# Moving the DMA transposes of a convolution-plus-SwiGLU kernel from ScalarE to SyncE, in sixths of a block

## The chip, the cores and the metric

The kernel runs on one core of a Trainium2 chip. The metric is device time in microseconds (us) of one execution, median of several runs. Before the change it is 1375.94 us (2 runs, 1375.61 to 1376.27).

Engines as the profile names them: PE is TensorE's matmul, PEld its weight load, ACT is ScalarE, DVE VectorE, POOL GpSimd, SP SyncE. A "q" at the end (SPq, ACTq) is the engine's sequencer, which issues DMAs and waits on semaphores.

## The reference, cut to what matters

```python
B, S, D = 8, 4096, 192; H, K = 8, 7          # 8 heads of 24 channels, 7 taps; Dff = 1536
w = softmax(weight)                          # (H, K)
y[b, s, h, :] = sum_k w[h, k] * x_pad[b, s + k, h, :]      # causal depthwise conv, per head
g, v = y @ w_gate, y @ w_val                 # (32768, 192) @ (192, 1536)
out = (g * sigmoid(g) * v) @ w_out           # (32768, 1536) @ (1536, 192)
```

## The kernel before

The work goes in units of 1024 tokens, two blocks of 512 each; there are 32 units. The FFN of a block runs over 12 chunks of 128 hidden channels, so a unit has 24 chunks, numbered s = 0 to 23. Each chunk has six gate/val matmuls ("gv", contraction over 192 channels in three parts of 64), a silu on ScalarE, a multiply on VectorE giving `h`, and, a few chunks later, matmuls of the down projection ("f2"). The f2 or conv matmuls of one chunk are called a burst. Between two bursts stands a relay: a nop on SyncE that waits for the last matmul before it and releases the first matmul of the next burst.

The conv of the next unit is done on TensorE as a Toeplitz matmul in four phases between the chunks. Its result stands with tokens on partitions, but gv needs channels on partitions. So it is staged in SBUF, written to DRAM, and read back with DMA transposes into `xq`.

```python
def emit_relay():                                  # orders TensorE bursts that swap PSUM banks
    relay[0] = nc.sync.nop(nofuse=True)            # SyncE waits for the last matmul of a burst;
    tc.add_manual_dep(relay[0].ins, last_mm[0].ins.name, SYNC, ...)
                                                   # the next burst's first matmul waits for this nop
# ... cut ...
def emit_to_dram(u):
    st = conv.pop(u)
    nc.gpsimd.tensor_copy(st[:, :, D:XD], st[:, :, 0:Q])
    dr = tc.dram_tile([2 * UG * G, XD], fp16, name=f"xc{u}")     # UG, G = 9, 57; XD = 256
    for i, lo in enumerate((0, Q)):
        nc.gpsimd.dma_start(                                      # 57 partitions x 9 rows of 512 B
            out=dr[i * UG * G : (i + 1) * UG * G, :].rearrange("(g r) d -> r g d", r=G),
            in_=st[lo : lo + G])
    return dr

def emit_transpose(dr):
    xq = xpool.tile([P, NQ, UT], fp16, tag="xq", name="xq")
    for q in range(NQ):                                           # 3 transposes of 1024 rows a unit
        nc.scalar.dma_start_transpose(out=xq[:, q, :], in_=dr[0:UT, q * Q : q * Q + P])
    return xq
# ... cut; in the chunk loop:
    emit_h(emit_gv(j, xqs[u], (b % UB) * TB), hlists[b])          # gv, silu, multiply
    if not tail: emit_f2(fj % 2, (c, c + 1), accs[fb], hlists[fb])  # one burst in every chunk
    if s in (4, 5, 8, 9): emit_conv(u + 1, s // 8, s % 2)
    emit_relay()
    if s == 9:  dr = emit_to_dram(u + 1)
    if s == 15: xqs[u + 1] = emit_transpose(dr)                   # on ScalarE's queue
```

## Time and profile before

| what | value | how it was read |
|---|---|---|
| span | 1378.4 us | page |
| unit period | 42.00 us | first write to DRAM of one unit to that of the next, mean of 30 |
| ScalarE stop in each unit | 12.0 to 14.1 us (31 stops) | timeline |
| first gate matmul | 41.8 us | timeline |
| mean granted TensorE clock | 0.861 | cores |

The timeline of ScalarE, last chunks ahead of the stop (start, duration, engine and line, operation, tiles; in brackets the idle time before and what ended it):

```profile
649.64 0.60 ACT L259 ACTIVATE sig<-gate 128x512 f16<-128x512 f32 x1 [0.44 <-PE gate L248]
650.17 0.48 ACT L298 COPY o_sb<-acc_8237 128x384 f32<-128x384 f32 x1
650.62 0.60 ACT L259 ACTIVATE sig<-gate 128x512 f16<-128x512 f32 x1
660.20 4.55 ACTq L237 DMA_TRANSPOSE xq<-xc_8416  x3
664.85 1.08 ACT L259 ACTIVATE sig<-gate 128x512 f16<-128x512 f32 x2 [13.64 <-issue]
```

ScalarE computes nothing from 651.2 to 664.9 us. Its queue is in order, and in front of the next silu stand three transposes. The chain of waits for the same stretch says why they started only at 660.2 us:

```profile
646.67 1.55 POOL xc_8416 L228
648.22 0.18 issue
648.40 11.74 DMA xc_8416<-stage
660.14 0.03 ACTq L237
660.17 0.04 issue
660.20 1.18 ACTq L237
661.38 0.03 issue
661.41 1.99 ACTq L237
663.39 0.03 issue
663.42 1.33 ACTq L237
```

They wait 11.7 us for the write to DRAM. The three issues then take 1.18, 1.99 and 1.33 us. TensorE runs dry behind this. The windows view of the same stop gives the granted clock in the column PEclk (ahead of it the busy time of PE, PEld, DVE, ACT, POOL; after it the DMA share and GB/s):

```profile
651.00:664.00 13.00, 2.44 (x35) 1.87 (x35) 1.02 (x2) 0.22 (x1) 2.57 (x4) 0.69 0.79 126
664.00:667.00 3.00, 1.36 (x5) 0.40 (x6) 1.28 (x2) 1.08 (x2) 0.00 (x0) 0.50 0.93 154
667.00:670.30 3.30, 3.30 (x32) 2.49 (x30) 1.14 (x2) 1.19 (x2) 0.00 (x0) 0.60 0.02 5
670.30:675.00 4.70, 4.70 (x70) 3.75 (x68) 2.98 (x5) 2.86 (x5) 0.00 (x0) 1.00 0.00 0
```

The clock is at half speed from 656.0 us, and back at 1.00 from 669.7 us. The Trainium skill, "TensorE: Matmul & The Clock Gate", section "What's actually happening", describes this: the clock falls to half after an idle window of about 3.4 us, and comes back after about as long a busy stretch. The trace agrees only in part. Full speed is back 4.1 us after the matmuls resumed at 665.5 us. But half speed began 2.1 us after the last matmul before the stop (653.9 us), too early for a whole idle window of 3.4 us.

### The profile page before, as it was taken

The page shows a single profiled execution, that of the slowest core. Times are in us where ns is not written, and L with a number is a line of the kernel's source. Part 1 is how long each engine was busy: PE and PEld are TensorE (multiplying, and loading weights), DVE is VectorE, ACT ScalarE, POOL GpSimd, SP SyncE. Part 2 cuts the span into 40 slices and gives each one's busy share as a digit, 9 for nine tenths or more (in the row PEclk, how much of TensorE's full clock was granted, in tenths as well). Part 3 has the DMA queues.
Part 4 walks back from the last instruction along what each step waited for, and adds up shares of the span by engine and source line. Part 5 has one row for each costly group of instructions (what it writes and reads, how often), then busy time and mean ns, then how long its engine had stood idle before and what let it go on. Part 6 is the DMA issues. An engine that isn't in the chain of part 4 may idle for free.

```text
span 1378.4 us, 28477 instructions
## 1 busy us (share of the span) xinstructions
PE 930.9 (68%) x11760; PEld 680.5 (49%) x11760; DVE 559.4 (41%) x857; ACT 536.8 (39%) x963; POOL 270.3 (20%) x310
## 2 busy tenths in 40 slices
PE   1676667866668766668666687666687666786668
PEld 0454445644446544456444465444465444554445
DVE  3343334433334433344333344333344333443335
ACT  0343334443334433344433344333344333443334
POOL 8211122202222101222012221012221112220110
PEclk9988888888889888898888898888998888888889
DMA  6324343234342243432343422344322444224421
GB/s 85 57 51 76 64 75 55 42 67 75 64 76 45 47 72 64 75 57 43 65 75 64 75 45 49 71 64 75 65 51 50 73 64 75 48 45 71 64 63 36
DMA packets 174418, 85.46 MB, mean 62 GB/s; under 512 B 162384, under 2 KB 165136, under 8 KB 174288
## 3 DMA queue, kind: packets, MB, share of 16 engines
q0 software_dynamic: 72768, 58.43, 22.4%
q10 hardware_dynamic: 101376, 25.18, 12.6%
q8 instruction: 92, 1.51, 0.4%
q14 instruction: 38, 0.31, 0.1%
q1 hardware_dynamic: 144, 0.03, 0.0%
HBM read 31.77 MB, written 41.98 MB: 54 GB/s over the span
## 4 chain that ended last, share of the span: by engine, by line
PE 39%; DMA 27%; issue 15%; ACTq 11%; DVE 5%; POOL 2%; ACT 2%; POOLq 0%; DVEq 0%; SPq 0%
PE val L248 17%; ACTq L237 11%; PE gate L248 7%; DVE h L261 2%; ACT sig L259 2%; DVE o_sb L299 1%; DMA xc_10122<-stage 1%; DMA xc_5574<-stage 1%; DMA xc_1026<-stage 1%; DMA xc_12964<-stage 1%; DMA xc_3868<-stage 1%; DMA xc_15238<-stage 1%; DMA xc_7848<-stage 1%; DMA xc_458<-stage 1%; DMA xc_8416<-stage 1%
## 5 line engine op out<-in xcount | busy, mean ns | idle before, releaser
L248 PE MATMUL gate<-xq,w_sb 64*128 64x512 f16 x2304 | 697.6, 403 | 369.5 <-ACT sig L259 349.5
L261 DVE TENSOR_TENSOR h<-sig,val 128x512 f16<-128x512 f16 x768 | 520.9, 686 | 809.0 <-ACT sig L259 776.1
L259 ACT ACTIVATE sig<-gate 128x512 f16<-128x512 f32 x768 | 455.2, 597 | 780.4 <-issue 413.2
L248 PE MATMUL val<-xq,w_sb 64*128 64x512 f16 x2304 | 667.8, 399 | 19.3 <-DVE h L261 14.9
L248 PEld LDWEIGHTS <-w_sb 64*128 64x128 f16 x4608 | 335.6, 98 | 518.9 <-issue 446.9
L274 PEld LDWEIGHTS <-h 64*128 64x128 f16 x6112 | 435.3, 98 | 151.7 <-issue 85.5
L300 POOL DMA_DIRECT2D out_dram<-o_sb x64 | 50.0, 781 | 831.8 <-ACT sig L259 672.3
L203 PEld LDWEIGHTS <-toep 64*128 64x128 f16 x1024 | 63.1, 95 | 20.6 <-DVE toep L150 17.8
L225 POOL COPY stage<-stage 128x576 f16<-128x576 f16 x32 | 21.7, 677 | 110.8 <-ACT stage L216 110.8
L203 PE MATMUL cps_171<-x_0_82,toep 64*128 64x216 f16 x8 | 2.0, 373 | 17.8 <-DMA wo_sb<-in_moe_w_out_dram 17.8
L95 POOL DMA_DIRECT2D x_1_84<-in_x_dram x16 | 12.4, 772 | 0.0
L97 POOL DMA_DIRECT2D x_1_84<-in_x_dram x16 | 11.8, 738 | 0.0
L97 POOL DMA_DIRECT2D x_0_82<-in_x_dram x16 | 11.4, 714 | 0.0
L101 POOL DMA_DIRECT2D x_1_84<-in_x_dram x16 | 9.3, 579 | 0.0
L101 POOL DMA_DIRECT2D x_0_82<-in_x_dram x16 | 9.1, 567 | 0.0
L259 ACT ACT_TABLE_LOAD x1 | 1.3, 1283 | 17.9 <-issue 17.9
L274 PE MATMUL acc_17072<-wo_sb,h 64*128 64x192 f16 x48 | 6.9, 273 | 0.5 <-DVE o_sb L299 0.5
L274 PE MATMUL acc_2292<-wo_sb,h 64*128 64x192 f16 x48 | 6.9, 273 | 0.5 <-DVE o_sb L299 0.5
L274 PE MATMUL acc_15368<-wo_sb,h 64*128 64x192 f16 x48 | 6.9, 273 | 0.5 <-DVE o_sb L299 0.5
L274 PE MATMUL acc_9682<-wo_sb,h 64*128 64x192 f16 x48 | 6.9, 273 | 0.5 <-DVE o_sb L299 0.5
L274 PE MATMUL acc_14230<-wo_sb,h 64*128 64x192 f16 x48 | 6.9, 272 | 0.5 <-DVE o_sb L299 0.5
L274 PE MATMUL acc_11956<-wo_sb,h 64*128 64x192 f16 x48 | 6.9, 272 | 0.5 <-DVE o_sb L299 0.5
(583 smaller groups left out, 1199.3 us busy)
## 6 DMA issues: line engine op xcount, KB each, us to landing
out_dram<-o_sb POOLq DMA_DIRECT2D x64, 384.0 KB, 4.1
x_0_82<-in_x_dram POOLq DMA_DIRECT2D x24, 192.0 KB, 10.8
x_1_84<-in_x_dram POOLq DMA_DIRECT2D x16, 216.0 KB, 10.9
x_1_84<-in_x_dram POOLq DMA_DIRECT2D x16, 192.0 KB, 11.2
x_0_82<-in_x_dram POOLq DMA_DIRECT2D x8, 216.0 KB, 11.1
w_sb<-in_moe_w_gate_dram POOLq DMA_DIRECT2D x12, 48.0 KB, 3.0
w_sb<-in_moe_w_val_dram POOLq DMA_DIRECT2D x12, 48.0 KB, 2.7
wo_sb<-in_moe_w_out_dram POOLq DMA_DIRECT2D x4, 144.0 KB, 3.6
```

The costliest lines, as they stand in the source:

```text
L95: nc.gpsimd.dma_start(out=x16[0:Q, :, :], in_=windows(t0, Q, UG))
L97: nc.gpsimd.dma_start(out=x16[Q:P, 0 : UG - 1, :], in_=windows(tb, Q, UG - 1))
L101: nc.gpsimd.dma_start(out=x16[Q : Q + last_rows, UG - 1, :], in_=x_flat[tl : tl + last_rows, :])
L203: mm = nc.tensor.matmul(conv["ps"][a][:, :, e, :], toep[lo : lo + Q, c * H + h, :], x16[lo : lo + Q, :, h * grp : (h + 1) * grp], start=(p ...
L225: nc.gpsimd.tensor_copy(st[:, :, D:XD], st[:, :, 0:Q])
L237: nc.scalar.dma_start_transpose(out=xq[:, q, :], in_=dr[0:UT, q * Q : q * Q + P])
L248: last_mm[0] = nc.tensor.matmul(ps[i], w_r[lo : lo + Q, q, ts(j, P)], xq[lo : lo + Q, q, t : t + TB], start=(q == 0), stop=(q == NQ - 1),)
L259: nc.scalar.activation(sj, ps[0], AF.Silu)
L261: nc.vector.tensor_tensor(hj, sj, ps[1], op=ALU.mult)
L274: mm = nc.tensor.matmul(acc[a][:, i, :], hlist[j][lo : lo + Q, ts(2 * a + i, P)], wo_r[lo : lo + Q, j, :], start=(j == 0 and half == 0 and ...
L299: nc.vector.tensor_copy(o_sb[:, 2:4, :], acc[1])
L300: nc.gpsimd.dma_start(out=out[t0 : t0 + TB, :].rearrange("(s p) d -> p s d", p=P), in_=o_sb)
```

## The change

Its intent is to take the wait and the issue of the transposes off ScalarE, to write and transpose block by block and earlier, and to shorten the start. A block is transposed in six pieces of 256 rows, called sixths; thirds and twelfths, further down, are pieces of 512 and 128 rows. The diff, cut to its core:

```diff
-    F2_LAG = 3
+    TR = 3                      # down projection in chunk triples: a burst in 2 of 3 chunks
+    F2_LAG = TR + 1
+    RP = TB // 2                # 256 rows a transpose
 # ... start: weights through SyncE's hardware queue as fp32, cast on ScalarE and GpSimd;
 #     Toeplitz matrix in two halves; Silu table loaded early ...
+        dr = tc.dram_tile([UG * G, XD], fp16, name=f"xc{b}")      # one DRAM tile a block
+        nc.sync.dma_start(out=dr.rearrange("(g r) d -> r g d", r=G),
+                          in_=conv[u][i * Q : i * Q + G])
+    def emit_transpose(b, i):                                     # i = 0 .. 5
+        r, q = i // NQ * RP, i % NQ
+        nc.sync.dma_start_transpose(
+            out=xqs[b][:, q, r : r + RP], in_=drs[b][r : r + RP, q * Q : q * Q + P])
 # ... in the chunk loop ...
-            if u + 1 < n_units and s in (4, 5, 8, 9):
-                emit_conv(u + 1, s // 8, s % 2)
+        if more and s in (0, 3, 6, 9):
+            emit_conv(u + 1, s // 6, s // 3 % 2)
+        if burst and live:
+            emit_relay()                                          # still a nop on SyncE
+        if g >= F2_LAG and fj == NCH - 2:
+            emit_store(fb, accs.pop(fb))                          # ahead of this chunk's multiply
+            if s in (3, 4, 9, 10):
+                emit_conv_out(u + 1, s // 6, s % 3)
+            if s in (11, 12):
+                emit_to_dram((u + 1) * UB + s - 11)
+            if 17 <= s < 17 + 2 * NQ:
+                emit_transpose((u + 1) * UB, s - 17)              # even block of the next unit
+        if live and s < 2 * NQ:
+            emit_transpose(u * UB + 1, s)                         # odd block of this unit
```

More of the change, by code (lines that the diff above doesn't have):

```diff
@@ L49 @@
     XD = D + Q
-    F2_LAG = 3
+    TR = 3
+    F2_LAG = TR + 1
+    RP = TB // 2
     SCALE = 1024.0
-    assert D == NQ * Q and NQ == 3
-    assert S % UT == 0 and UT <= 2 * UG * G and UT > (2 * UG - 1) * G
+    assert D == NQ * Q and NQ == 3 and UB == 2 and UG * G >= TB
+    assert S % UT == 0 and (UG - 1) * G < TB <= UG * G
     assert G + pad <= Q
-    assert NCH % 2 == 0 and H % 4 == 0 and 2 * UG * grp <= 512
+    assert NCH % TR == 0 and UB * NCH == 24 and H == 8 and 2 * UG * grp <= 512
     n_blocks = NT // TB
@@ L66 @@
     spool = ctx.enter_context(tc.tile_pool(name="stage", bufs=2))
-    xpool = ctx.enter_context(tc.tile_pool(name="xq", bufs=2))
+    xpool = ctx.enter_context(tc.tile_pool(name="xq", bufs=3))
     hpool = ctx.enter_context(tc.tile_pool(name="ffn", bufs=2))
@@ L72 @@
     apool = ctx.enter_context(tc.tile_pool(name="acc", bufs=1, space=bass.MemoryType.PSUM))
-    last_rows = UT - ((2 * UG - 1) * G - pad)
+    last_rows = TB - ((UG - 1) * G - pad)
     x16s = []
@@ L95, in emit_fetch @@
             nc.gpsimd.dma_start(out=x16[0:Q, :, :], in_=windows(t0, Q, UG))
-        tb = t0 + UG * G
+        tb = t0 + TB
         nc.gpsimd.dma_start(
@@ L103, in emit_fetch @@
         )
-    emit_fetch(0)
+    man = tc.manual_schedule(engines={EN.PE, EN.SP, EN.Activation, EN.DVE, EN.Pool})
+    ctx.enter_context(man)
     wraw = const_pool.tile([P, H, K], fp32, tag="wraw", name="wraw")
@@ L111 @@
     )
+    emit_fetch(0)
+    w_st = wpool.tile([P, NQ, Dff], fp32, tag="w_st", name="w_st")
+    wo_st = wpool.tile([P, NCH, D], fp32, tag="wo_st", name="wo_st")
+    w_r = wpool.tile([P, NQ, Dff], fp16, tag="w_sb", name="w_sb")
+    wo_r = wpool.tile([P, NCH, D], fp16, tag="wo_sb", name="wo_sb")
+    FS = Dff // 4
+    wg_v = moe_w_gate.rearrange("(q p) f -> p q f", p=Q)
+    wv_v = moe_w_val.rearrange("(q p) f -> p q f", p=Q)
+    wo_v = moe_w_out.rearrange("(c p) d -> p c d", p=P)
+    for f in range(0, Dff, FS):
+        fs = slice(f, f + FS)
+        cs = slice(f // P, (f + FS) // P)
+        nc.sync.dma_start(out=w_st[0:Q, :, fs], in_=wg_v[:, :, fs])
+        nc.sync.dma_start(out=w_st[Q:P, 0 : NQ - 1, fs], in_=wv_v[:, 1:NQ, fs])
+        nc.sync.dma_start(out=w_st[Q:P, NQ - 1, fs], in_=wv_v[:, 0, fs])
+        nc.sync.dma_start(out=wo_st[:, cs, :], in_=wo_v[:, cs, :])
+    diag = const_pool.tile([P, G], i32, tag="diag", name="diag")
+    for lo in (0, Q):
+        nc.gpsimd.iota(diag[lo : lo + Q], pattern=[[-1, G]], base=0, channel_multiplier=1)
+    band = const_pool.tile([P, H, 2, G], fp16, tag="band", name="band")
+    nc.gpsimd.memset(band, 0.0)
+    toep = const_pool.tile([P, H, 2, P], fp16, tag="toep", name="toep")
+    nc.gpsimd.memset(toep, 0.0)
+    masks = []
+    for k in range(K):
+        mask = const_pool.tile([P, G], u16, tag=f"mask{k}", name=f"mask{k}")
+        nc.vector.tensor_scalar(mask, diag, scalar1=k, scalar2=None, op0=ALU.is_equal)
+        masks.append(mask)
     wmax = const_pool.tile([P, H], fp32, tag="wmax", name="wmax")
@@ L118 @@
     nc.scalar.activation(wexp, wexp, AF.Exp)
+    warm = const_pool.tile([P, H, K], fp32, tag="warm", name="warm")
+    nc.scalar.activation(warm, wexp, AF.Silu)
     wsum = const_pool.tile([P, H], fp32, tag="wsum", name="wsum")
     nc.vector.tensor_reduce(wsum, wexp, axis=AX.X, op=ALU.add)
-    nc.vector.tensor_scalar(wsum, wsum, scalar1=1e-9, scalar2=None, op0=ALU.add)
+    nc.vector.tensor_scalar(
+        wsum, wsum, scalar1=1e-9, scalar2=1.0 / SCALE, op0=ALU.add, op1=ALU.mult
+    )
     nc.vector.reciprocal(wsum, wsum)
@@ L126 @@
     )
-    nc.vector.tensor_scalar(wn, wn, scalar1=SCALE, scalar2=None, op0=ALU.mult)
-    whl = const_pool.tile([P, 2, H, K], fp16, tag="whl", name="whl")
-    nc.vector.tensor_copy(whl[:, 0], wn)
-    nc.vector.tensor_tensor(whl[:, 1], wn, whl[:, 0], op=ALU.subtract)
-    diag = const_pool.tile([P, G], i32, tag="diag", name="diag")
-    for lo in (0, Q):
-        nc.gpsimd.iota(diag[lo : lo + Q], pattern=[[-1, G]], base=0, channel_multiplier=1)
-    band = const_pool.tile([P, 2 * H, G], fp16, tag="band", name="band")
@@ L137 @@
-    nc.gpsimd.memset(band, 0.0)
-    toep = const_pool.tile([P, 2 * H, P], fp16, tag="toep", name="toep")
-    nc.gpsimd.memset(toep, 0.0)
-    wflat = whl.rearrange("p c h k -> p (c h) k")
-    for k in range(K):
-        mask = const_pool.tile([P, G], u16, tag=f"mask{k}", name=f"mask{k}")
-        nc.vector.tensor_scalar(mask, diag, scalar1=k, scalar2=None, op0=ALU.is_equal)
-        nc.vector.copy_predicated(
-            band,
-            mask.unsqueeze(1).to_broadcast([P, 2 * H, G]),
-            wflat[:, :, k : k + 1].to_broadcast([P, 2 * H, G]),
-        )
@@ L150 @@
-    nc.vector.tensor_copy(toep[0:Q, :, 0:G], band[0:Q])
-    nc.vector.tensor_copy(toep[Q:P, :, Q : Q + G], band[Q:P])
-    w_r = wpool.tile([P, NQ, Dff], fp16, tag="w_sb", name="w_sb")
-    wo_r = wpool.tile([P, NCH, D], fp16, tag="wo_sb", name="wo_sb")
-    FS = Dff // 4
-    wo_v = moe_w_out.rearrange("(c p) d -> p c d", p=P)
-    for f in range(0, Dff, FS):
-        for lo, w, first in ((0, moe_w_gate, 0), (Q, moe_w_val, 1)):
-            wv = w.rearrange("(q p) f -> p q f", p=Q)
-            for q in range(NQ):
-                nc.gpsimd.dma_start(
-                    out=w_r[lo : lo + Q, q, f : f + FS],
-                    in_=wv[:, (q + first) % NQ, f : f + FS],
-                )
-        c0, c1 = f // P, (f + FS) // P
-        nc.gpsimd.dma_start(out=wo_r[:, c0:c1, :], in_=wo_v[:, c0:c1, :])
+    whl = const_pool.tile([P, H, 2, K], fp16, tag="whl", name="whl")
@@ new lines @@
+    nc.vector.tensor_copy(whl[:, :, 0], wn)
+    nc.vector.tensor_tensor(whl[:, :, 1], wn, whl[:, :, 0], op=ALU.subtract)
+    for h in range(0, H, 4):
+        hs = slice(h, h + 4)
+        for k in range(K):
+            nc.vector.copy_predicated(
+                band[:, hs].rearrange("p h c m -> p (h c) m"),
+                masks[k].unsqueeze(1).to_broadcast([P, 8, G]),
+                whl[:, hs, :, k : k + 1]
+                .rearrange("p h c k -> p (h c) k")
+                .to_broadcast([P, 8, G]),
+            )
+        nc.vector.tensor_copy(toep[0:Q, hs, :, 0:G], band[0:Q, hs])
+        nc.vector.tensor_copy(toep[Q:P, hs, :, Q : Q + G], band[Q:P, hs])
@@ L169, with emit_weight_cast @@
+    def emit_weight_cast(i):
+        fs = slice(i * FS, (i + 1) * FS)
+        cs = slice(i * FS // P, (i + 1) * FS // P)
+        nc.scalar.copy(w_r[:, :, fs], w_st[:, :, fs])
+        nc.gpsimd.tensor_copy(wo_r[:, cs, :], wo_st[:, cs, :])
+    emit_weight_cast(0)
     SYNC = mybir.DependencyInfo(mybir.DependencyClass.Sync, mybir.DependencyReason.DATA)
@@ L204, in emit_conv @@
                         conv["ps"][a][:, :, e, :],
-                        toep[lo : lo + Q, c * H + h, :],
+                        toep[lo : lo + Q, h, c, :],
                         x16[lo : lo + Q, :, h * grp : (h + 1) * grp],
@@ L211, in emit_conv, with emit_conv_out, emit_dup, emit_to_dram @@
                     after_relay(mm)
-    def emit_conv_out(u, fill):
-        for a in range(2):
-            d0 = (4 * fill + 2 * a) * grp
-            nc.scalar.mul(
-                conv[u][:, :, d0 : d0 + 2 * grp],
-                conv["ps"][a].rearrange("p g e d -> p g (e d)"),
-                1.0 / SCALE,
-            )
-    def emit_to_dram(u):
-        st = conv.pop(u)
-        nc.gpsimd.tensor_copy(st[:, :, D:XD], st[:, :, 0:Q])
-        dr = tc.dram_tile([2 * UG * G, XD], fp16, name=f"xc{u}")
-        for i, lo in enumerate((0, Q)):
-            nc.gpsimd.dma_start(
-                out=dr[i * UG * G : (i + 1) * UG * G, :].rearrange("(g r) d -> r g d", r=G),
-                in_=st[lo : lo + G],
-            )
-        return dr
-    def emit_transpose(dr):
-        xq = xpool.tile([P, NQ, UT], fp16, tag="xq", name="xq")
-        for q in range(NQ):
-            nc.scalar.dma_start_transpose(
-                out=xq[:, q, :], in_=dr[0:UT, q * Q : q * Q + P]
-            )
-        return xq
-    def emit_gv(j, xq, t):
+    def emit_conv_out(u, fill, a):
+        d0 = (4 * fill + 2 * a) * grp
+        nc.scalar.mul(
+            conv[u][:, :, d0 : d0 + 2 * grp],
+            conv["ps"][a].rearrange("p g e d -> p g (e d)"),
+            1.0 / SCALE,
+        )
+    def emit_dup(u):
+        nc.gpsimd.tensor_copy(conv[u][:, :, D:XD], conv[u][:, :, 0:Q])
+    drs = {}
+    def emit_to_dram(b):
+        u, i = divmod(b, UB)
+        dr = tc.dram_tile([UG * G, XD], fp16, name=f"xc{b}")
+        nc.sync.dma_start(
+            out=dr.rearrange("(g r) d -> r g d", r=G),
+            in_=conv[u][i * Q : i * Q + G],
+        )
+        drs[b] = dr
+    xqs = {}
+    def emit_transpose(b, i):
+        if i == 0:
+            xqs[b] = xpool.tile([P, NQ, TB], fp16, tag="xq", name="xq")
+        r, q = i // NQ * RP, i % NQ
+        nc.sync.dma_start_transpose(
+            out=xqs[b][:, q, r : r + RP], in_=drs[b][r : r + RP, q * Q : q * Q + P]
+        )
+    def emit_gv(j, xq):
         ps = [
@@ L250, in emit_gv @@
                     w_r[lo : lo + Q, q, ts(j, P)],
-                    xq[lo : lo + Q, q, t : t + TB],
+                    xq[lo : lo + Q, q, :],
                     start=(q == 0),
@@ L255, in emit_gv, with emit_silu, emit_h @@
         return ps
-    def emit_h(ps, hlist):
+    def emit_silu(ps):
         sj = hpool.tile([P, TB], fp16, tag="sig", name="sig", bufs=3)
         nc.scalar.activation(sj, ps[0], AF.Silu)
-        hj = hpool.tile([P, TB], fp16, tag="h", name="h", bufs=8)
+        return sj
+    def emit_h(sj, ps, hlist):
+        hj = hpool.tile([P, TB], fp16, tag="h", name="h", bufs=9)
         nc.vector.tensor_tensor(hj, sj, ps[1], op=ALU.mult)
@@ L302, in emit_store @@
         )
-    with tc.manual_schedule(engines={EN.PE, EN.SP, EN.Activation, EN.DVE, EN.Pool}):
-        for fill in range(2):
-            for phase in range(2):
-                emit_conv(0, fill, phase)
-                emit_relay()
-            emit_conv_out(0, fill)
-        xqs = {0: emit_transpose(emit_to_dram(0))}
-        if n_units > 1:
-            emit_fetch(1)
-        hlists, accs = {}, {}
-        ns = NCH * UB
-        for g in range(n_blocks * NCH + F2_LAG):
-            b, j = divmod(g, NCH)
-            u, s = divmod(g, ns)
-            if b < n_blocks:
-                if j == 0:
-                    hlists[b] = []
-                emit_h(emit_gv(j, xqs[u], (b % UB) * TB), hlists[b])
-            if g >= F2_LAG:
-                fb, fj = divmod(g - F2_LAG, NCH)
-                if fj == 0:
-                    accs[fb] = [
-                        apool.tile([P, 2, D], fp32, tag=f"acc{i}", name=f"acc{i}")
-                        for i in range(2)
-                    ]
-                tail = fb == n_blocks - 1 and fj >= NCH - F2_LAG - 1
-                if not tail:
-                    c = fj // 2 * 2
-                    emit_f2(fj % 2, (c, c + 1), accs[fb], hlists[fb])
-                elif g == n_blocks * NCH:
-                    for jf in range(NCH - F2_LAG - 1, NCH):
-                        emit_f2_full(jf, accs[fb], hlists[fb][jf])
-            if u + 1 < n_units and s in (4, 5, 8, 9):
-                emit_conv(u + 1, s // 8, s % 2)
-            if b < n_blocks:
-                emit_relay()
-            if g >= F2_LAG and fj == NCH - 1:
-                emit_store(fb, accs.pop(fb))
-                del hlists[fb]
-            if u + 1 < n_units:
-                if s in (5, 9):
-                    emit_conv_out(u + 1, s // 8)
-                if s == 9:
-                    dr = emit_to_dram(u + 1)
-                if s == 10 and u + 2 < n_units:
-                    emit_fetch(u + 2)
-                if s == 15:
-                    xqs[u + 1] = emit_transpose(dr)
-                    xqs.pop(u - 1, None)
@@ new lines @@
+    for fill in range(2):
+        for phase in range(2):
+            emit_conv(0, fill, phase)
+            emit_relay()
+        for a in range(2):
+            emit_conv_out(0, fill, a)
+        if fill == 0:
+            emit_dup(0)
+    emit_to_dram(0)
+    for i in range(2 * NQ):
+        emit_transpose(0, i)
+    emit_to_dram(1)
+    for i in range(1, 4):
+        emit_weight_cast(i)
+    if n_units > 1:
+        emit_fetch(1)
+    hlists, accs = {}, {}
+    ns = NCH * UB
+    for g in range(n_blocks * NCH + F2_LAG):
+        b, j = divmod(g, NCH)
+        u, s = divmod(g, ns)
+        more = u + 1 < n_units
+        live = b < n_blocks
+        if live:
+            if j == 0:
+                hlists[b] = []
+            ps = emit_gv(j, xqs[b])
+            sj = emit_silu(ps)
+        burst = False
+        if g >= F2_LAG:
+            fb, fj = divmod(g - F2_LAG, NCH)
+            if fj == 0:
+                accs[fb] = [
+                    apool.tile([P, 2, D], fp32, tag=f"acc{i}", name=f"acc{i}")
+                    for i in range(2)
+                ]
+            t, half = divmod(fj, TR)
+            tail = fb == n_blocks - 1 and t >= NCH // TR - 2
+            if half < 2 and not tail:
+                emit_f2(half, range(t * TR, (t + 1) * TR), accs[fb], hlists[fb])
+                burst = True
+            elif tail and g == n_blocks * NCH:
+                for jf in range((NCH // TR - 2) * TR, NCH):
+                    emit_f2_full(jf, accs[fb], hlists[fb][jf])
+        if more and s in (0, 3, 6, 9):
+            emit_conv(u + 1, s // 6, s // 3 % 2)
+            burst = True
+        if burst and live:
+            emit_relay()
+        if g >= F2_LAG and fj == NCH - 2:
+            emit_store(fb, accs.pop(fb))
+        if live:
+            emit_h(sj, ps, hlists[b])
+        if g >= F2_LAG and fj == NCH - 1:
+            del hlists[fb], xqs[fb]
+        if more:
+            if s in (3, 4, 9, 10):
+                emit_conv_out(u + 1, s // 6, s % 3)
+            if s == 5:
+                emit_dup(u + 1)
+                if u + 2 < n_units:
+                    emit_fetch(u + 2)
+            if s in (11, 12):
[4 more added lines that the diff above has]
+            emit_transpose(u * UB + 1, s)
```

## The prediction

> **What bounds the kernel now.** In the timeline of one unit (1024 tokens, 24 chunks) the period is about 42 us. The in-order ScalarE queue stops for 13.8 us in each unit: the three DMA transposes stand on it in front of the next silu, and they wait for the write of the staged conv result to DRAM (11 to 12 us from issue to landing; the chain of waits shows that DMA, then 4.5 us of transpose issue: 1.18, 1.99, 1.33 us). The wait list shows it as 413 us of ScalarE "issue" idle in 31 stops, 350 us of TensorE waiting for sig, up to 12 us each. After each stop the granted clock is 0.50 for about 6.5 us (windows), where a chunk takes 1.9 us, not 1.0; about 3 us a unit. So 31 units lose about 15 us each, 460 us or more in all. Left are 27 us a unit: 24 chunks of 1.01 us, four conv phases of 0.37 us, two block ends of 0.75 us where the down projection waits for the o_sb copies. TensorE's own work is 24.9 us (gate/val pairs step 0.215 us, down pairs 0.083 us). First gate matmul: 41.8 us.
>
> **What the change does.**
> 1. Transposes leave ScalarE. Gone: the 13.8 us stop and the slow clock, 15 us x 31: the main term, all on the critical path.
> 2. Relay nops, DRAM writes and transposes now share SyncE's in-order queue. A transpose that waits there holds the relay behind it, and TensorE stops one or two bursts later. The write of 513 rows of 512 B is issued in chunk 11, its transposes in chunk 17, about 6 us later. The Trainium skill, "DMA: Bandwidth & Descriptors", section "Why a DMA increments its semaphore by 16 and not by 1", lets a hardware-queue DMA use only as many engines (at most 16) as divide its slowest dimension; 57 rows would give 3. Then each engine has 171 rows; at 40 to 65 ns a row (estimate; the packets of the writes in this trace average 62 to 69 ns) a write takes 9 to 13 us, and the second queues behind it. I estimate 1 to 5 us of SyncE stall a unit. No run shows it yet.
> 3. The last sixth is issued after chunk 22's burst and should land about 2.4 us later (estimate: 3.2 us at least for the large ones, less issue): about 0.7 us of wait at a unit's start.
> 4. Triples: same matmuls, fewer switches, but burstless chunks of 0.65 us run into the silu-multiply loop (2.03 us per two chunks). About neutral. Earlier store and split conv copies save perhaps 0.5 us a unit.
> 5. Start: half the write, smaller transposes, Silu table loaded early: gate at about 31 us, 10 us saved.
>
> **Sum.** 33 us of start and cold clock, 32 units of 26.5 us, 3 us of tail: 884 us if SyncE never blocks. With 1.3 us a unit of blocking: 925 us. Range 855 to 1060. Faster by over 2%: 0.98; within: 0.01; slower: 0.01.
>
> **What would show it.** No ScalarE stop of over 3 us; granted clock near 1.0 after the start; unit period 26 to 30 us; landing time of the writes to DRAM (6 us or less: item 2 wrong; 9 us or more: right), and waits of TensorE's first burst matmul for SyncE; first gate matmul near 31 us.
>
> **What would make it wrong.** Writes on few engines so slow that SyncE stops over 3 us a unit, bringing back the slow clock (1100 us or more); weights on the hardware queue that delay the first conv or the casts.

## The result, and the profile after

The kernel after takes 1081.01 us (2 runs, 1079.25 to 1082.78) against 1375.94 us. The ratio is 0.7857, 95% interval 0.7801 to 0.7912. Here and below a ratio is the mean time of one kernel's fast runs over that of the other's of the same rounds, so it is not quite the ratio of the medians quoted. The direction was right, but the time lies 156 us above the point and 21 us above the range.

| what | before | after |
|---|---|---|
| unit period | 42.00 us | 32.26 us |
| transposes issued in a unit, mean issue time | 3, 1.54 us | 12, 1.30 us |
| longest wait of ScalarE once the chunks run | 14.1 us | 4.7 us |
| longest gap between TensorE's matmuls there | about 12 us | 2.6 us |
| mean granted clock | 0.861 | 0.987 |
| first gate matmul | 41.8 us | 38.0 us |

The stop on ScalarE is gone and the slow clock nearly so, as predicted, though not to the mark that the prediction set ("no ScalarE stop of over 3 us"): 17 waits of ScalarE are 3.2 to 4.7 us long. The windows view of one unit after shows PEclk at 1.00:

```profile
509.00:512.00 3.00, 2.65 (x30) 1.33 (x25) 2.06 (x3) 1.66 (x3) 0.00 (x0) 1.00 0.15 42
512.00:517.00 5.00, 4.57 (x61) 3.00 (x62) 3.15 (x5) 2.51 (x6) 0.79 (x1) 1.00 0.40 125
517.00:526.00 9.00, 7.08 (x88) 3.94 (x87) 4.15 (x7) 3.47 (x6) 0.00 (x0) 1.00 0.26 64
526.00:535.00 9.00, 8.46 (x116) 5.03 (x111) 5.07 (x8) 5.45 (x10) 3.37 (x5) 1.00 0.44 86
535.00:540.40 5.40, 5.31 (x86) 4.06 (x86) 2.96 (x6) 3.83 (x7) 0.00 (x0) 1.00 0.72 92
```

What came in place of the stop stands in the page's part 4, the chain that ended last, shares of the span by engine and by line. L268 is the transpose, L255 the write to DRAM:

```profile
PE 43%; SPq 32%; DMA 8%; DVE 7%; issue 4%; ACT 4%; POOL 0%; POOLq 0%; ACTq 0%; DVEq 0%
```

A third of the chain now runs through SyncE's sequencer. The timeline of SyncE over one unit shows what it does there:

```profile
509.06 0.25 SPq L255 DMA_DIRECT2D xc_8578<-stage  x1
509.36 2.58 SPq L255 DMA_DIRECT2D xc_8592<-stage  x1
516.57 7.92 SPq L268 DMA_TRANSPOSE xq<-xc_8578  x6
526.60 8.40 SPq L268 DMA_TRANSPOSE xq<-xc_8592  x6
```

Six transposes of 256 rows take 7.9 us to issue, with relays between them. The list of the line's instructions (minimum, median and maximum of the duration in ns; first and last start in us) puts one at 1.2 us, nearly what one of 1024 rows took before. Before and after, one unit each:

```profile
L237 ACTq DMA_TRANSPOSE xq<-xc_8416 x3: 1177/1332/1986, 660.2 to 663.4; - x3
```

```profile
L268 SPq DMA_TRANSPOSE xq<-xc_1686 x6: 1174/1240/1625, 139.7 to 146.8; - x6
```

So a quarter of the rows costs about the same issue. Twelve of them hold SyncE for 15.6 us of each unit. A chunk takes about 1.0 us. In 12 of 24 chunks SyncE must issue one transpose, and in 10 of these 12 also pass on a relay. The list of waits shows the two ways in which this reaches TensorE (total us, times, longest): the loads of the bursts' weights wait for the relay, L205, and gate matmuls wait for a transpose.

```profile
PEld L307 <- SPq L205: 145.4, 168, 3.1
PEld L227 <- SPq L205: 25.9, 56, 1.6
```

These waits of weight loads for a relay come to 171 us. Weight loads overlap with matmuls: the idle time of the matmuls themselves that a relay ended is 68 us (120 times). Waits of gate matmuls for transposed data are 52 us in all, 15 us of them at the start. In the unit above the sixth transpose was issued at 523.32 us, and 2.32 us later the chain shows it landed while a gate matmul waited:

```profile
520.75 1.18 SPq L268
521.98 1.23 SPq L268
523.32 2.32 DMA xq<-xc_8578
525.68 0.37 PE gate L278
```

The rival in the prediction, a write confined to few engines, can be read as well. While only the write ran, from 510.5 to 514.5 us, its hardware queue took 20.8% of 16 engines' time, that is 3.3 engines:

```profile
DMA packets 483, 0.25 MB, mean 61 GB/s; under 512 B 3, under 2 KB 483, under 8 KB 483
## 3 DMA queue, kind: packets, MB, share of 16 engines
q1 hardware_dynamic: 483, 0.25, 20.8%
```

The two writes' 1026 packets of 512 B took 28 ns each on average and ran from 509.88 to 519.47 us. That makes 1026 x 28 ns / 9.6 us = 3.0 at a time on average, which fits three engines. But 28 ns a row is about half of what I had estimated, and the first write was through by the time its transposes started in chunk 17.

### The profile page after: what moved, and what is told of

The parts are those of the page before. It is cut to its first block, busy times and chain, and to the rows that moved or that the text cites. A ratio compares the mean times of both kernels' runs of the same rounds, so it can differ in the third digit from the quotient of the medians.

```text
span 1077.4 us, 28716 instructions
## 1 busy us (share of the span) xinstructions
PE 910.0 (84%) x11752; PEld 562.7 (52%) x11752; DVE 572.8 (53%) x865; ACT 550.1 (51%) x968; POOL 146.5 (14%) x222
## 4 chain that ended last, share of the span: by engine, by line
PE 43%; SPq 32%; DMA 8%; DVE 7%; issue 4%; ACT 4%; POOL 0%; POOLq 0%; ACTq 0%; DVEq 0%
SPq L268 24%; PE gate L278 17%; PE val L278 9%; SPq L255 8%; DVE h L294 4%; ACT sig L289 4%; DVE o_sb L332 2%; DVE band L174 1%; DMA xc_220<-stage 1%; DMA xc_229<-stage 1%; DMA xq<-xc_16634 0%; DMA xq<-xc_11455 0%; SPq L205 0%; DMA xq<-xc_6851 0%; DMA xq<-xc_6276 0%
## 5 line engine op out<-in xcount | busy, mean ns | idle before, releaser
L294 DVE TENSOR_TENSOR h<-sig,val 128x512 f16<-128x512 f16 x768 | 526.2, 687 | 443.5 <-ACT sig L289 386.2
L278 PE MATMUL gate<-xq,w_sb 64*128 64x512 f16 x2304 | 645.6, 382 | 53.1 <-DMA xq<-xc_220 15.4
L278 PE MATMUL val<-xq,w_sb 64*128 64x512 f16 x2304 | 634.7, 380 | 18.1 <-DVE h L294 13.1
L307 PEld LDWEIGHTS <-h 64*128 64x128 f16 x6096 | 297.2, 95 | 198.7 <-SPq L205 145.4
L278 PEld LDWEIGHTS <-w_sb 64*128 64x128 f16 x4608 | 263.2, 95 | 250.7 <-issue 107.7
L227 PEld LDWEIGHTS <-toep 64*128 64x128 f16 x1024 | 49.1, 97 | 59.1 <-SPq L205 25.9
L307 PE MATMUL acc_325<-wo_sb,h 64*128 64x192 f16 x48 | 5.3, 243 | 3.2 <-SPq L205 3.2
L307 PE MATMUL acc_4067<-wo_sb,h 64*128 64x192 f16 x48 | 5.3, 243 | 2.9 <-SPq L205 2.9
L307 PE MATMUL acc_9246<-wo_sb,h 64*128 64x192 f16 x48 | 5.8, 258 | 2.1 <-SPq L205 2.1
L307 PE MATMUL acc_14425<-wo_sb,h 64*128 64x192 f16 x48 | 5.7, 256 | 2.1 <-SPq L205 2.1
L307 PE MATMUL acc_15577<-wo_sb,h 64*128 64x192 f16 x48 | 5.8, 258 | 1.8 <-SPq L205 1.8
L307 PE MATMUL acc_4642<-wo_sb,h 64*128 64x192 f16 x48 | 5.3, 243 | 2.4 <-SPq L205 2.4
L307 PE MATMUL acc_9821<-wo_sb,h 64*128 64x192 f16 x48 | 5.8, 258 | 1.4 <-SPq L205 1.4
```

The costliest lines, as they stand in the source:

```text
L227: mm = nc.tensor.matmul(conv["ps"][a][:, :, e, :], toep[lo : lo + Q, h, c, :], x16[lo : lo + Q, :, h * grp : (h + 1) * grp], start=(phase ...
L278: last_mm[0] = nc.tensor.matmul(ps[i], w_r[lo : lo + Q, q, ts(j, P)], xq[lo : lo + Q, q, :], start=(q == 0), stop=(q == NQ - 1),)
L294: nc.vector.tensor_tensor(hj, sj, ps[1], op=ALU.mult)
L307: mm = nc.tensor.matmul(acc[a][:, i, :], hlist[j][lo : lo + Q, ts(2 * a + i, P)], wo_r[lo : lo + Q, j, :], start=(j == 0 and half == 0 and ...
```

## The experiments

Theory A: each transpose issue holds SyncE for about 1.2 us whatever its size, in front of the relays. Theory B: the writes on three engines land late and everything waits for data. Theory C: the chunk triples and the silu-multiply loop bound the unit. All kernels gave correct results. They were timed against the kernel before in the same rounds; the kernel after was not timed again with them, so differences from 1081 us are differences of medians from separate jobs.

| run | edit | us | ratio to before (95%) | unit period, us |
|---|---|---|---|---|
| after | | 1081.0 | 0.786 (0.780 to 0.791) | 32.26 |
| e1 | relay on GpSimd | 1043.1 | 0.757 (0.754 to 0.760) | 31.21 |
| e2 | thirds | 937.0 | 0.681 (0.680 to 0.682) | 27.81 |
| e3 | write split 48 + 9 | 1036.3 | 0.752 (0.750 to 0.754) | 31.30 |
| e4 | even sixths a chunk earlier | 1055.2 | 0.767 (0.765 to 0.768) | 31.45 |
| e5 | e2 + e3 | 905.6 | 0.658 (0.657 to 0.660) | 26.94 |
| e6 | e5 + relay on GpSimd | 921.0 | 0.669 (0.668 to 0.671) | 27.50 |
| e7 | e5 + pairs | 901.3 | 0.656 (0.654 to 0.657) | 26.89 |
| e8 | before + transposes on SyncE | 1195.6 | 0.868 (0.865 to 0.871) | 36.12 |
| e9 | sixths, both paths freed | 924.4 | 0.672 (0.671 to 0.674) | 27.54 |
| e10 | e7 + earlier transposes | 888.7 | 0.646 (0.645 to 0.648) | 26.48 |
| e11 | e5 + earlier transposes | 901.6 | 0.655 (0.654 to 0.657) | 26.82 |
| e12 | twelfths | 1587.5 | 1.154 (1.150 to 1.159) | 48.04 |

### e1_relay_pool: the relay off SyncE

```diff
-        relay[0] = nc.sync.nop(nofuse=True)
+        relay[0] = nc.gpsimd.nop(nofuse=True)
```

> Change against the kernel after: the relay nop alone moves from SyncE to GpSimd; all DMA issues stay. Theory A (each transpose holds SyncE for about 1.2 us whatever its size, and the relays that TensorE waits for stand behind 12 of them a unit): the waits of TensorE for SyncE (about 170 us) vanish, the late last sixth (about 50 us) too, since SyncE no longer stops for relays: 860 to 910 us. Theory B (the writes to DRAM on few engines land late and everything waits for data): no gain, 1060 to 1090 us, with the waits moved to DMA. Theory C (chunk triples and the silu-multiply loop bound the unit): at most 30 us gained, 1050 us or more.

Measured: 1043 us. The waits for SyncE's relay did go (weight loads wait 30 us for GpSimd's instead), yet theory A as I had put it missed by over 130 us. The list of waits shows where they went (first line TensorE, second line SyncE's own):

```profile
PE gate L278 <- DMA xq<-xc: 86.9, 81, 12.9
```

```profile
SPq L268 <- DMA xc<-stage: 100.1, 33, 5.2
```

The chain of one unit's end in e1 is now a chain of issues and a landing:

```profile
527.63 3.43 SPq L268
531.11 1.25 SPq L268
532.40 1.24 SPq L268
533.68 1.24 SPq L268
534.97 2.38 DMA xq<-xc
```

The six issues cost twice. Besides standing in front of the relays, they stand in series between the write to DRAM and the next unit's first gate matmuls. In e1 the first write was issued at 519.1 us, the first transpose at 524.9 us, and the last one landed at 537.3 us. That is 18 us for a path that has the 13 chunks from 11 to 24 to hide in, 13 to 14 us. So theory A became A2: two paths, both priced in issues. The write takes part in the second one: SyncE waits 100 us in all for it to land, about 3 us a unit, and the transpose issues took 2.67 and 3.43 us while the second write was still running (to 529.4 us); with split writes (e5) the longest issue is 2.10 us.

### e2_thirds: half as many issues

```diff
-    RP = TB // 2
+    RP = TB                                   # 512 rows
-            if 17 <= s < 17 + 2 * NQ:
-                emit_transpose((u + 1) * UB, s - 17)
+            if s in (17, 19, 21):
+                emit_transpose((u + 1) * UB, (s - 17) // 2)
-        if live and s < 2 * NQ:
-            emit_transpose(u * UB + 1, s)
+        if live and s in (0, 2, 4):
+            emit_transpose(u * UB + 1, s // 2)
```

> Change against the kernel after: three transposes of 512 rows a block (chunks 17, 19, 21 and 0, 2, 4) in place of six of 256 rows. Theory A (issue cost fixed near 1.2 us): each issue stays at 1.1 to 1.4 us, SyncE is held half as long, total 960 to 1010 us. If the issue cost goes with the rows (my prediction's assumption): each issue takes about 2.4 us and the total stays at 1060 to 1100 us. Theory B: no change.

Measured: 937 us, 144 us less than after and more than A asked for. Twice the rows do not cost more to issue:

```profile
L268 SPq DMA_TRANSPOSE xq<-xc x192: 1122/1148/2170, 33.7 to 909.6; - x192
```

The edit also brings the last piece of an even block from chunk 22 to chunk 21. e4, below, moves all six sixths a chunk earlier and gains 26 us, so that may be a part of the 144 us, but not most of it.

### e3_write16: the write over more engines

```diff
+        dv = dr.rearrange("(g r) d -> r g d", r=G)
+        for r0, r1 in ((0, 48), (48, G)):
+            nc.sync.dma_start(out=dv[r0:r1], in_=conv[u][i * Q + r0 : i * Q + r1])
```

> Change against the kernel after: each write to DRAM is split into 48 and 9 of its 57 partitions, so that the larger part can use 16 engines; two issues in place of one. Theory B (landing time of the write on three engines bounds): packets of 512 B overlap on many engines, the two writes end about 6 us earlier, total 1000 us or less. Theory A: the writes end earlier but the total stays within 30 us of 1081; at most the 2.6 us for which SyncE is held by the second write goes down.

Measured: 1036 us. In the trace the 1026 packets now end 2.9 us after they begin rather than 9.6, about 14 at a time (39 ns each), and from 525.8 to 528.3 us the queue holds 92.8% of 16 engines:

```profile
q1 hardware_dynamic: 973, 0.48, 92.8%
```

The gain is 45 us, more than A's 30 and less than B's 80. The writes on three engines are a real part of the loss, but not the main part. In this trace the gain came through the first path: the waits of gate matmuls for transposes after the start stay as they were (36 us, 37 in the kernel after), while those of weight loads for relays fall from 171 to 131 us. The second write, whose one issue had held SyncE for 2.58 us, now takes two issues of 0.67 and 0.41 us (medians).

### e4_early: even sixths in chunks 16 to 21

```diff
-            if 17 <= s < 17 + 2 * NQ:
-                emit_transpose((u + 1) * UB, s - 17)
+            if 16 <= s < 16 + 2 * NQ:
+                emit_transpose((u + 1) * UB, s - 16)
```

> Change against the kernel after: the six transposes of an even block go out in chunks 16 to 21, not 17 to 22. Theory A says that the wait at a unit's start for the last sixth (about 1.7 us a unit, 52 us in all) shrinks by about 1 us a unit: 1035 to 1060 us. Theory B: the first sixth now waits for the write, the same time as after or longer.

Measured: 1055 us, inside A's range and against B. One chunk earlier bought 0.8 us a unit. The waits of gate matmuls for transposes after the start fall from 37 to 1 us, and those of weight loads for relays rise from 171 to 208 us: part of the loss changed its path.

### e5_thirds_write16 and e6_thirds_write16_pool: both edits, then the relay too

> Change against the kernel after: e2 and e3 together (three transposes of 512 rows a block; each write to DRAM split into 48 and 9 partitions). Revised theory A2: the fixed 1.2 us of a transpose issue costs twice, on SyncE in front of the relays and in the chain write to DRAM, six issues, landing before a unit's first gate matmul; the write on three engines adds to both (it holds SyncE for 2.6 us in the second write and slows the first two transposes behind it). With thirds the second write's hold is what is left (1.0 us of TensorE wait for SyncE a unit): 890 to 920 us. Rival C (silu-multiply loop with triples alone is left): 925 us or more, as e2.

> Change against e5: the relay moves to GpSimd as well. A2: in e5 SyncE is held for at most 1.2 us at a time and only in six chunks, so little is left to gain: within 15 us of e5. If relays behind transposes still bind in e5: 20 to 40 us faster than e5.

Measured: 905.6 us and 921.0 us. e5 is what A2 said, and SPq has 1% of its chain. In e6 the relay on GpSimd costs 15 us (A2 had said "within 15 us"), since it now stands behind GpSimd's own work (31.5 us of waits of the f2 weight loads for POOLq). With the right number of issues SyncE is the better place for it.

### e7_thirds_write16_pairs: down projection in pairs again

```diff
-    TR = 3
+    TR = 2
-        if g >= F2_LAG and fj == NCH - 2:
+        if g >= F2_LAG and fj == NCH - 1:
```

> Change against e5: down projection in chunk pairs (a burst in every chunk, as before the change), store after chunk 11's burst. C (triples cost time through the burstless chunks, 3.16 us per three chunks against 3.03): 10 to 25 us faster than e5. If triples pay (fewer switches, room for the store): 10 to 40 us slower. A2 says nothing on it.

Measured: 901.3 us, only 4 us under e5, which is neither of the expected sizes. This comparison was not clean, because transposes still make up 7% of e7's chain (3% of e5's). e10 against e11 repeats it without that wait.

### e8_before_sp: the move without the rest, on the kernel before

```diff
-            nc.scalar.dma_start_transpose(
+            nc.sync.dma_start_transpose(
-                if s == 15:
+                if s == 20:
-    relay[0] = nc.sync.nop(nofuse=True)
+    relay[0] = nc.gpsimd.nop(nofuse=True)
```

> Change against the kernel before: the three transposes of 1024 rows go out on SyncE in chunk 20 and the relay moves to GpSimd; nothing else. It asks what taking the transposes off ScalarE is worth alone. The stop of 13.8 us and the slow clock go, but the writes still land about 11.7 us after issue (chunk 22) and three issues and the landing follow, so that the first gate matmul of a unit waits 1 to 4 us: 940 to 1030 us. If the gain of the change came mainly from its other parts: over 1150 us.

Measured: 1195.6 us, a miss by 166 us, and above the 1150 us from which I had wanted to conclude that the gain came mainly from the other parts. The writes (issued by GpSimd from 604.4 us) took until 617.7 us, then came three issues, and the last transpose landed 3.5 us after its issue:

```profile
618.99 1.96 SPq L237
621.00 3.49 DMA xq<-xc
624.53 0.58 PE gate L248
```

A unit's start still waits about 4 us (121 us of waits of gate matmuls after the start, in 31 units), at the upper end of the 1 to 4 us that I had put down. What I had left out is the slow clock that follows the wait (170 us at half speed, mean clock 0.930) and the relay on GpSimd, for which matmuls wait 46 us. So the move, with the relay on GpSimd and the issue five chunks later, is worth 180 us, 61% of the 295 us that the change gained; the line at 1150 us was drawn wrongly. The other 115 us need the other parts of the change; I did not separate the faster write from the new chunk schedule there.

### e9_sixths_free: sixths kept, both paths freed

The edits of e1 and e3, and:

```diff
-            if 17 <= s < 17 + 2 * NQ:
-                emit_transpose((u + 1) * UB, s - 17)
+            if 15 <= s < 15 + 2 * NQ:
+                emit_transpose((u + 1) * UB, s - 15)
```

> Change against the kernel after: sixths stay (12 issues a unit, about 15 us of SyncE), but both paths on which they cost are freed: the relay goes to GpSimd, each write is split into 48 and 9 partitions, and the even block's sixths go out in chunks 15 to 20. A2: the issues themselves cost nothing then, 905 to 940 us (e6, with half the issues, was 921). Rival (many small transposes cost by themselves, by DMA contention or more packets): 960 us or more.

Measured: 924.4 us. Its twelve issues still take 16.3 us of SyncE in each unit, twice as long as the six of e6 (8.0 us). The transposes of e9 and then of e6:

```profile
L267 SPq DMA_TRANSPOSE xq<-xc x384: 1103/1243/2566, 27.3 to 895.6; - x192
```

```profile
L267 SPq DMA_TRANSPOSE xq<-xc x192: 1122/1261/2474, 27.3 to 881.7; - x192
```

The time differs from e6's by 3 us (e6 has its transposes in chunks 17, 19 and 21). Both kernels have the relay on GpSimd, and the waits of their f2 weight loads for it are the same, 31 us. So issue time costs next to nothing by itself here. It costs only where it stands ahead of a relay or between the write and the next unit. This is the run that settles A2 against the rival that small transposes cost by themselves.

### e10_pairs_early and e11_triples_early: transposes in chunks 15, 17, 19

```diff
-            if s in (17, 19, 21):
-                emit_transpose((u + 1) * UB, (s - 17) // 2)
+            if s in (15, 17, 19):
+                emit_transpose((u + 1) * UB, (s - 15) // 2)
```

> Change against e7: the even block's three transposes go out in chunks 15, 17, 19 in place of 17, 19, 21. In e7 a unit still starts with a wait of about 1.1 us for the last transpose. A2: that wait goes, 860 to 880 us. If the write has not landed by chunk 15, SyncE stops there and the gain is under 10 us.

> Change against e5: the same earlier transposes, with the chunk triples. The trace of e5 shows the same wait of about 1.1 us at a unit's start: 865 to 890 us. Against e10 it is the clean comparison of triples and pairs: C expects e10 to be 10 to 25 us faster.

Measured: 888.7 us and 901.6 us. Both gained less than expected (13 us on e7, 4 us on e5): the list of waits of e5 has no more than 14 us of gate matmuls waiting for transposes, the start included, so the gap that I had read in one unit's timeline did not stand for all units. Pairs beat triples by 12.9 us, inside C's 10 to 25. The timeline of e11 shows silus in threes, 1.14, 0.87 and 1.15 us apart. In e10 they alternate between 0.98 and 1.04 us. The chain of e10 (page, part 4) is nearly all TensorE:

```profile
PE 93%; DVE 2%; SPq 2%; issue 2%; DMA 1%; POOL 0%; POOLq 0%; ACT 0%; ACTq 0%; DVEq 0%
```

e10 is the fastest kernel here: 888.7 us, 0.646 of before.

### e12_twelfths: the suspected cost doubled

```diff
-    RP = TB // 2
+    RP = TB // 4                              # 128 rows, two a chunk in the same chunks
```

> Change against the kernel after: twelve transposes of 128 rows a block, two a chunk in the same chunks. The suspected cost is doubled. Fixed issue cost of about 1.2 us: SyncE is held for 2.4 us in each of 12 chunks, about 14 us a unit more, 1450 to 1550 us. Cost that goes with the rows: 0.6 us each, the total stays at 1060 to 1100 us.

Measured: 1587.5 us. An issue of 128 rows takes as long as one of 256:

```profile
L268 SPq DMA_TRANSPOSE xq<-xc x768: 1094/1224/3141, 31.1 to 1556.4; - x192
```

Twelve more issues lengthen the unit by 48.04 - 32.26 = 15.8 us, 1.3 us each. The total came out above my range. What I had not counted is the slow clock: in this trace it is at half speed for 498 us (mean 0.843).

## Why the prediction was wrong

- **Item 1, the stop on ScalarE: right.** The stops of 12 to 14 us are gone and the mean clock is 0.987. e8 shows that the move, with the relay on GpSimd, gives 180 us without the rest.
- **Item 2, SyncE's blocking: the step that failed.** The place was right (SyncE's in-order queue, relays behind transposes), but the term was mis-sized. It was "1 to 5 us of SyncE stall a unit", entered in the sum as 1.3 us. It was priced as waiting for the write's data, and the twelve transpose issues themselves were not priced at all. I took for granted that an issue of a quarter of the rows is short. The runs show 1.2 us at 128 and 256 rows, 1.1 at 512, about 1.3 at 1024: 15.6 us of SyncE in each unit. The trace of before held 1.33 us for 1024 rows, but only one size, so a fixed cost could not be told from one that goes with the rows. A sum that held both cases would have carried 12 x 1.2 us. The unit became 32.3 us, not 27.8; that is 4.46 us x 32 = 143 us of the 156 us by which the point was missed. e2, e12 and e9 show the cause.
- **Item 2, the write on three engines: mechanism right, size off.** Three engines, as the Trainium skill says in "DMA: Bandwidth & Descriptors", section "Why a DMA increments its semaphore by 16 and not by 1", and 3.0 packets at a time in the trace. But a row takes 28 ns, not 40 to 65. The 62 to 69 ns behind that estimate were not of the writes alone: the mean over all packets of GpSimd's queue, 4 to 4608 bytes each, is 62 ns from 648.4 to 660.2 us. By the test that the prediction set itself (landing in 6 us or less: wrong; 9 us or more: right) the result is split: half of the packets had begun 5.2 us after the first write's issue, and the last ended 10.1 us after the second's. e3 puts the worth of the writes at 45 us.
- **Item 3, the late last sixth: landing right, start wrong.** It lands 2.3 us after issue (2.4 predicted). It is issued late because the sixths before it pile up on SyncE, so gate matmuls wait about 37 us in all after the start; 0.7 us x 31 had made 22. That path matters far more once the relays are freed (e1).
- **Item 4, triples about neutral: close.** They cost 12.9 us of about 900 (e11 against e10), for the reason given there.
- **Item 5, the start: off by 7 us.** First gate matmul at 38.0 us, not 31. Six issues of 1.2 us stand in series there too, but they are not all of it: the time is 36.4 us with three issues (e2), 35.4 us with the split write (e3) and 31.5 us with both (e5).
- **The sum without blocking was sound.** It said 884 us; e5 measures 906, e11, with the earlier transposes, 902, and e10, with pairs in place of the triples of the change, 889.

What stays open: how the 144 us of e2 divide between the two paths, since they trade places as soon as one is freed (e1, e4). The single gains of e1, e3 and e4 must not be added up.

## What to carry to other kernels

Price a DMA issue by its count and not by its bytes until two sizes have been timed. Cutting a transpose in pieces multiplied the issue time here (e2, e12), and everything behind it on the in-order queue paid, semaphore relays included. When a queue carries both signals and transfers, also look at the serial chain from producer to consumer: freeing the signals (e1) gained a quarter of what fewer issues gained, because the same issues stood on a second path. Before a write moves to a hardware queue, look at how its outermost dimension divides; here splitting 57 into 48 and 9 cut two writes from 9.6 to 2.9 us.

## What the Trainium skill lacked or had wrong

- "DMA: Bandwidth & Descriptors", section "Why a DMA increments its semaphore by 16 and not by 1": its one figure for issuing a DMA transpose from HBM is 631 sequencer cycles for small tiles on "previous generations", the older side of a comparison with a later chip. At the 1.2 GHz that "Trainium Kernel Development and Optimization" gives SyncE, that is 0.53 us (an estimate). It names no number of rows. The runs show more than twice that, and nearly no dependence on size: 1.22 us (median) for 128 rows, 1.18 for 256, 1.15 for 512 and 1.33 for 1024, all 128 columns of 2-byte elements.
- "Trainium Kernel Development and Optimization", section "Key Constraints": "issuing from several engines concurrently only saves the sequencer's issue time". No run here tests that, but issue time can be what counts: here the weight loads of the bursts waited 171 us for relays on the queue that issues the DMAs.
- "DMA: Bandwidth & Descriptors", the same section, on how many engines a DMA uses: right on the hardware queue (57 partitions, 3.0 packets at a time; 48 and 9 partitions, about 14). It does not say that a second such write then holds the issuing sequencer, here for 2.58 us against 0.25 us for the first.
- "TensorE: Matmul & The Clock Gate", section "What's actually happening": it gives half clock as the state after at least one idle window of about 3.4 us. The runs differ: a window about half busy was enough. In the kernel after, no gap between matmuls is over 2.6 us once the chunks run, yet the clock fell to half eight times between the first chunk and the last, for 3.41 us each. Before the first fall the longest gap was 1.0 us (windows view; PE busy 1.50 of 3.41 us, then PEclk 0.50):

```profile
362.34:365.75 3.41, 1.50 (x18) 0.74 (x20) 0.69 (x1) 0.42 (x1) 0.00 (x0) 1.00 0.18 39
365.75:369.16 3.41, 3.41 (x32) 2.11 (x30) 1.22 (x2) 1.19 (x2) 0.00 (x0) 0.50 0.09 19
```

All fourteen traces, from the first gate matmul to the last, were cut into windows of 3.41 us at the clock's own changes. All 180 falls followed a window in which matmuls were busy 0.54 of the time or less, and the clock never stayed full after a window below 0.42. Full speed came back only after windows busy 0.80 or more, and half speed never lasted after a window above 0.88. The shares are rough, since the ends of matmuls are modelled.
